# A causal convolution and a token mixer on one core: batch 0's loads, the softmax, the weight casts and the remainder stores

## The chip, the core and the metric

The kernel runs on one core of a Trainium2 chip. That core has a matrix engine (PE, whose weight loads are shown as PEld), a vector engine (DVE), a scalar engine (ACT), GpSimd (POOL), an engine that only issues transfers (SP), and 16 DMA engines that move data between the chip's memory and the core. The metric is device microseconds of one execution; less is better.

## The reference

The input x has 8 batches of 4224 tokens with 192 values each. First comes a causal convolution of 7 taps. Each of 8 heads (24 values each) has its own taps, which are the softmax of its row of `weight`. Then comes a token mixer without softmax:

```
w   = softmax(weight)                      # 8 heads x 7 taps
y   = sum_k w[h,k] * x[s-6+k, h*24:...]    # zeros before token 0
q,k = y @ w_q, y @ w_k                     # 192 -> 64
out = relu((q @ k.T / 8) @ y) @ w_out
```

Since nothing stands between `q @ k.T` and the product with y, the kernel computes `q @ (k.T @ y)`, and `k.T @ y` as `w_k.T @ (y.T @ y)`. With G = y.T y (192 by 192) it forms M = w_k.T G / 8 (64 by 192), and then relu(q M) w_out.

## The kernel before, in words

A batch is cut into two halves of 2112 tokens, and each half into 18 chunks of 122 outputs. A chunk of x lies on 128 partitions (6 tokens of history and 122 tokens), as bf16 in `XW`, which has room for 6 batches. GpSimd issues the loads of x (line 252 for whole chunks, line 273 for the short last chunk), and the DMA converts from float32 on the way. `rows` issues one load of some chunks of one half.

Per batch the stages are:

- Y: the convolution, as a product with a banded matrix per head (`BAND`, line 433), and the evacuation from PSUM to `Y`. `YC` clears the unused rows of the last chunk.
- T: transposes on DVE, 32 by 32 (line 787), and Q: the product with w_q (line 498).
- G: the sum of y.T y over 18 chunks in PSUM bank 7 (lines 526 to 528), its evacuation `GS`, a transposed block (line 546), and MM, which makes M (lines 558 to 563).
- Z: relu(q M), three products of 512 columns for each of 4 blocks of tokens (line 597), and a small remainder of 64 tokens per half (line 600).
- O: the product with w_out (lines 640 and 642; 634 and 635 for the remainder), the evacuation to `OUT`, and the store from SP (line 670). A block's store is 768 KB, the remainder's 96 KB.

PSUM is emptied by ACT or DVE (lines 787 to 795). The order of all this work is written out ahead of time by a planner in the kernel. `KEYS` gives each stage a first key and a width in units of a batch. `CLOCK` holds the times at which the planner takes data to be there: the four groups of batch 0 (`x0`), the band matrix, the weights, and batch 1 onwards (`x`: the first time and the distance between batches). A job that could start now goes by its key; otherwise the job that can start first goes. The planner also decides whether ACT or DVE does each evacuation. On the chip each engine runs its list strictly in order and waits at semaphores, so a job whose data come later than planned holds everything behind it on that engine.

The start is outside the planner: SP loads `weight` spread to 128 partitions (line 282) and w_q (line 288), GpSimd issues batch 0 in four groups of chunks (0 to 2, 3 to 8, 9 to 14, 15 to 17, both halves), 128 partitions compute the same softmax (lines 335 to 345), five predicated copies shift each partition's row of taps to its place (line 358), and four copies write the band (line 371). SP loads w_k and w_out (line 310) behind a wait for batch 0's second group. PE runs 60 matmuls on zeros meanwhile (line 405). The casts of w_k and w_out to bf16 are eight planner jobs (`job_w`), on ACT or DVE. DVE clears the parts of `XW` that loads don't fill, for batches 1 to 5, in two instructions (lines 399 and 400).

Of the kernel before, what the change touches and what calls it, by code (L numbers as in the profile page):

```python
# [14 lines left out]
    "Y": (-1.0, 0.64), "Q": (-0.3, 1.4), "G": (0.06, 0.63), "Z": (0.73, 1.5), "O": (1.59, 0.9),  # L15
# [3 lines left out]
    "x0": (5.0, 6.6, 9.2, 11.6), "band": 6.5, "wq": 6.5, "wk": 11.0, "wo": 12.0, "x": (12.0, 12.0),  # L19
    "store": 5.0, "now": 0.05, "hold": 1.5,  # L20
# [138 lines left out]
def bass_lightweight_conv__then__hypermixer_token_mlp_kernel(  # L159
# [61 lines left out]
    W_F = sbuf("w_f", [128, H, KC], F32)  # L221
    W_MX = sbuf("w_mx", [128, H], F32)
    W_EX = sbuf("w_ex", [128, H, KC], F32)
    W_SM = sbuf("w_sm", [128, H], F32)
    SHIFT = sbuf("shift", [128, H, 56], BF16)
    BITS = sbuf("bits", [128, 1], I32)
# [5 lines left out]
    GROUPS = [[(0, 3), (3, 9), (9, 15), (15, 18)]] + [[(0, 9), (9, 18)]] * (B - 1)  # L232
# [26 lines left out]
    def load(b, c0, c1, grp, deps=()):  # L259
        full = min(c1, NCK - 1)  # L260
        for half in range(2):
            c = c0
            if half == 0 and c == 0:
                rows(b, 0, 0, 16, 128, 1, grp, deps)
                rows(b, 0, 0, 6, 16, 1, grp, deps)
                c = 1
            rows(b, half, c, 0, 128, full - c, grp, deps)
        if c1 == NCK:
            hi = 6 + LAST + (4 if b < B - 1 else 0)
            at = (b * S + (NCK - 1) * CW - 6) * D  # L270
            P.dma(
                "pool",
                lambda e: e.dma_start(
                    XW[0:hi, b % NX, :, NCK - 1, :],
                    bass.AP(x_t, at, [[D, hi], [HALF * D, 2], [1, D]]),
                ),
                grp, list(deps) + z_short[:1] if b == 0 else deps,
            )
# [3 lines left out]
        lambda e: e.dma_start(W_F[:, :, :], bass.AP(w_t, 0, [[0, 128], [1, H * KC]])),  # L282
# [17 lines left out]

    for g, (c0, c1) in enumerate(GROUPS[0]):
        load(0, c0, c1, xg[0][g])
        if g == 0:
            bits = pool(lambda e: e.iota(BITS[:, :], [[0, 1]], base=127, channel_multiplier=-1))

# [11 lines left out]
    for s, (src, wd) in enumerate(((wk_t, DH), (wo_t, D))):  # L317
        wload(2 * s, 0, 128, src, 0, wd, wl[s + 1], [xg[0][1]])
        wload(2 * s + 1, 0, 64, src, 128, wd, wl[s + 1], ())
        wload(2 * s + 1, 64, 128, src, 128, wd, wl[s + 1], ())  # L320


    mask = PS[:, 7, 0:5].bitcast(I32)
    z_mask = []
    for j in range(5):
        z_mask.append(dve(
            lambda e, j=j: e.tensor_scalar(mask[:, j : j + 1], BITS[:, :], j, 1,
# [3 lines left out]

    def bc(ap, n):
        return ap.unsqueeze(2).to_broadcast([128, H, n])

    d = dve(lambda e: e.tensor_reduce(W_MX[:, :], W_F[:, :, :], AX.X, ALU.max), [wg])
    d = dve(
        lambda e: e.tensor_tensor(W_EX[:, :, :], W_F[:, :, :], bc(W_MX[:, :], KC), ALU.subtract),
        [d],
    )
# [63 lines left out]
    def warm(e):  # L403
        for i in range(60):
            last = e.matmul(PS[:, 0, 0:128], WARM[:, :], WARM[:, :], start=True, stop=True)
# [515 lines left out]
```

## Time and profile before

| | |
|---|---|
| median of the runs | 177.39 us (176.98, 177.39, 178.78) |
| the profiled execution, its own time | 179.23 us |
| its span, first to last instruction | 177.5 us |
| busy in the span | PE 86%, ACT 78%, DVE 64%, POOL 27% |
| mean granted clock of PE | 0.943 |
| last matmul's end, last transfer's end | about 165.7 us, about 176.7 us |

The views below count time from the span's start. In a table of stretches each row has a stretch and its length, then the busy time and number of instructions of PE, PEld, DVE, ACT and POOL, then the clock that PE was granted, the mean number of packets in flight per DMA engine (1.00 is one on each of the 16 at all times; it can exceed 1, because an engine holds more than one), and the rate in GB/s. In a timeline each row has a start, a length, the engine ("SPq" is SP issuing a transfer), the line, the operation, its output and input, its shape, how many were merged into the row, and in brackets how long the engine had been idle and what ended that. "x12" is a count.

### The profile page before, as it was taken

How to read it: one execution, taken by the hardware profiler on the slowest of the kernel's cores; microseconds unless marked ns; L12 is line 12 of the kernel's file. 1: busy time of each engine (PE TensorE's matmuls, PEld its weight loads, DVE VectorE, ACT ScalarE, POOL GpSimd, SP SyncE). 2: the span in 40 equal slices, each digit the busy share in tenths (PEclk: the TensorE clock that was granted, in tenths of full speed). 3: DMA queues.
4: the chain of work that ended last, by engine and by line, in shares of the span. 5: the costliest groups of instructions: out<-in, count | busy, mean ns of one | idle time of the engine just before them, and what ended most of it. 6: DMA issues, size and time to landing. Idle time of an engine off the chain costs nothing.

```text
span 177.5 us, 4686 instructions
## 1 busy us (share of the span) xinstructions
PE 152.8 (86%) x1958; PEld 112.8 (64%) x1980; DVE 113.1 (64%) x228; ACT 138.1 (78%) x255; POOL 47.6 (27%) x71
## 2 busy tenths in 40 slices
PE   7739869999999999999999999999599999999300
PEld 7717647667666776677667766776367778766200
DVE  2725828969976686758676867686725863896100
ACT  2346596989999998999899989998767986899400
POOL 7999999999505000000000000000000000000000
PEclk9965978999999999999999999999969999999975
DMA  3999999999999999999999999555640585497980
GB/s 57 130 170 189 206 189 192 190 194 190 261 285 293 262 213 335 250 327 213 329 248 331 216 333 304 199 187 198 219 178 11 215 317 187 158 392 230 388 292 23
DMA packets 48084, 40.38 MB, mean 227 GB/s; under 512 B 37696, under 2 KB 40384, under 8 KB 48064
## 3 DMA queue, kind: packets, MB, share of 16 engines
q0 software_dynamic: 36576, 13.65, 64.7%
q1 hardware_dynamic: 11488, 26.44, 41.3%
q8 instruction: 15, 0.25, 0.5%
q14 instruction: 5, 0.04, 0.1%
HBM read 27.77 MB, written 25.95 MB: 303 GB/s over the span
## 4 chain that ended last, share of the span: by engine, by line
PE 71%; DMA 8%; ACT 7%; issue 3%; POOL 2%; SPq 1%; DVE 1%; ACTq 0%; POOLq 0%
PE ps L640 13%; PE ps L433 11%; PE ps L642 11%; PE ps L597 9%; PE ps L498 8%; PE ps L526 7%; PE ps L527 6%; DMA xw<-in_x_dram 4%; DMA wst<-in_moe_w_out_dram 4%; PE ps L528 4%; POOL xw L252 2%; ACT qt L789 2%; ACT y L789 2%; SPq L310 1%; ACT o_sb L789 1%
## 5 line engine op out<-in xcount | busy, mean ns | idle before, releaser
L789 ACT CAST y<-ps 128x864 bf16<-128x864 f32 (+7 forms) x94 | 50.7, 596 | 8.2 <-PE ps L433 7.9
L789 ACT COPY o_sb<-ps 128x768 f32<-128x768 f32 (+1 forms) x64 | 48.6, 776 | 4.4 <-PE ps L642 3.2
L793 DVE TENSOR_SCALAR zt<-ps 128x512 bf16<-128x512 f32 x54 | 36.8, 683 | 21.6 <-PE ps L597 19.5
L252 POOL DMA_DIRECT2D xw<-in_x_dram x52 | 41.1, 810 | 8.9 <-issue 8.1
L433 PE MATMUL ps<-xw,band 128*128 128x432 bf16 (+2 forms) x144 | 36.1, 354 | 8.6 <-ACT y L789 2.9
L640 PE MATMUL ps<-wo,zt 128*128 128x192 bf16 x256 | 42.5, 248 | 0.3
L642 PE MATMUL ps<-wo,zt 128*128 128x384 bf16 x128 | 41.8, 326 | 0.0
L526 PE MATMUL ps<-y 128*128 128x192 bf16 x144 | 35.6, 254 | 0.9 <-issue 0.2
L787 DVE STREAM_TRANSPOSE yb<-y 128x576 int32<-128x576 int32 x48 | 33.8, 749 | 2.7 <-ACT y L795 2.7
L527 PE MATMUL ps<-y 128*128 128x192 bf16 x144 | 35.4, 254 | 0.0
L640 PEld LDWEIGHTS ps<-wo,zt 128*128 128x128 bf16 x256 | 26.2, 115 | 11.5 <-ACT o_sb L789 3.6
L528 PE MATMUL ps<-y 128*128 128x128 bf16 x144 | 32.4, 225 | 0.0
L597 PE MATMUL ps<-qt,m_sb 128*128 128x512 bf16 x74 | 26.1, 380 | 1.1 <-issue 1.0
L792 ACT ACTIVATE zt<-ps 128x512 bf16<-128x512 f32 x42 | 24.4, 620 | 0.3 <-PE ps L597 0.3
L433 PEld LDWEIGHTS ps<-xw,band 128*128 128x128 bf16 x144 | 12.3, 104 | 16.4 <-ACT y L789 4.6
L527 PEld LDWEIGHTS ps<-y 128*128 128x128 bf16 x144 | 14.6, 101 | 8.4 <-issue 0.7
L526 PEld LDWEIGHTS ps<-y 128*128 128x128 bf16 x144 | 14.6, 102 | 5.4 <-issue 1.1
L789 ACT CAST qt<-ps 128x576 bf16<-128x576 f32 (+1 forms) x21 | 11.7, 585 | 7.2 <-PE ps L498 7.0
L498 PE MATMUL ps<-yb,wq 32*64 32x288 bf16 x768 | 16.0, 294 | 0.5
L789 DVE CAST y<-ps 128x864 bf16<-128x864 f32 (+4 forms) x14 | 10.9, 789 | 8.0 <-PE ps L433 7.8
L789 DVE CAST qt<-ps 128x234 bf16<-128x234 f32 (+1 forms) x27 | 10.3, 414 | 8.1 <-PE ps L498 8.1
L528 PEld LDWEIGHTS ps<-y 128*128 128x128 bf16 x144 | 14.5, 101 | 0.1
(72 smaller groups left out, 121.9 us busy)
## 6 DMA issues: line engine op xcount, KB each, us to landing
out_dram<-o_sb SPq DMA_DIRECT2D x30, 768.0 KB
xw<-in_x_dram POOLq DMA_DIRECT2D x21, 384.0 KB, 27.3
xw<-in_x_dram POOLq DMA_DIRECT2D x7, 432.0 KB, 24.9
out_dram<-o_sb SPq DMA_DIRECT2D x4, 384.0 KB
xw<-in_x_dram POOLq DMA_DIRECT2D x4, 288.0 KB, 7.4
out_dram<-o_sb SPq DMA_DIRECT2D x8, 96.0 KB
xw<-in_x_dram POOLq DMA_DIRECT2D x8, 42.0 KB, 14.7
xw<-in_x_dram POOLq DMA_DIRECT2D x3, 96.0 KB, 7.3
```

The costliest lines, as they stand in the source:

```text
L252: return e.dma_start(XW[lo:hi, b % NX, half, c : c + n, :], bass.AP(x_t, at, [[D, hi - lo], [CW * D, n], [1, D]]),)
L433: last = e.matmul(PS[:, k + j, 0 : 48 * n], BAND[:, h, :], rhs, start=True, stop=True)
L498: last = e.matmul(PS[64 * h : 64 * h + 64, bk + i, 0:288], WQ[r, j, :], rhs, start=j == 0, stop=j == 5, skip_group_check=True)
L526: e.matmul(PS[:, 7, 0:192], y[:, 0:128], y[:, 0:192], start=c == 0, **fl)
L527: e.matmul(PS[:, 7, 192:384], y[:, 256:384], y[:, 192:384], start=False, **fl)
L528: return e.matmul(PS[:, 7, 384:512], y[:, 128:256], y[:, 128:256], start=False, **fl)
L597: return e.matmul(PS[:, bk, :], m[:, parts[k] : parts[k] + 128], q, start=True, stop=True)
L640: e.matmul(o[:, 192 * h : 192 * h + 192], z[:, h, cols], WO1[:, :], start=h == 0, stop=False, **kw)
L642: last = e.matmul(o[:, 0:384], z[:, 2, cols], WO2[:, :], start=False, stop=True, **kw)
L787: return e.transpose(o, i)
L789: return e.copy(o, i) if eng == "act" else e.tensor_copy(o, i)
L793: return e.tensor_scalar(o, i, 0.0, None, op0=ALU.max)
```

## The change

- **Loads of batch 0.** Seven groups, each of one half: chunks 1 to 5 of half 0, chunks 0 to 4 of half 1, chunk 0 of half 0, then 6 to 10, 5 to 9, 11 to 17, 10 to 17. A new job `job_y1` convolves 2, 3, 4 or 8 heads of one half into one PSUM bank. The first half of batch 1's loads is issued ahead of the weight casts, the second half behind them.
- **Softmax.** `weight` is loaded on 8 partitions, one head each; the maximum is subtracted and the sum taken inside the exponential; each head's row is placed in its own column block by a mask, and one matmul with ones spreads the 8 rows to 128 partitions.
- **Weights.** SP's loads of w_k and w_out wait for the fourth new group. The eight casts are GpSimd instructions in its list, no longer planner jobs.
- **Clearing.** `M_SB` is cleared by DVE instead of GpSimd; the unfilled parts of `XW` by GpSimd, batch by batch ahead of that batch's loads, instead of by DVE at once.
- **Filler.** 16 matmuls on zeros ahead of the spreading one and 20 behind it, instead of 60; and in the planner's first 16 us, where it expects PE to be idle for over 0.3 us, matmuls on zeros in a free bank.
- **Stores.** The remainder's store is two transfers of 64 rows, one per half, instead of one of 2 by 64 rows. In the last batch the remainder goes ahead of block 3, and only block 3 is stored in two parts (before: blocks 2 and 3); those parts lie together in `OUT`.
- **Planner.** All `KEYS` and `CLOCK` have new values.

```diff
 KEYS = {
-    "Y": (-1.0, 0.64), "Q": (-0.3, 1.4), "G": (0.06, 0.63), "Z": (0.73, 1.5), "O": (1.59, 0.9),
+    "Y": (-0.83, 0.98), "Q": (-0.34, 1.7), "G": (0.16, 0.5), "Z": (0.87, 1.34), "O": (1.6, 0.8),
 }
 CLOCK = {
-    "x0": (5.0, 6.6, 9.2, 11.6), "band": 6.5, "wq": 6.5, "wk": 11.0, "wo": 12.0, "x": (12.0, 12.0),
-    "store": 5.0, "now": 0.05, "hold": 1.5,
+    "x0": (6.0, 7.2, 7.5, 8.7, 9.9, 11.8, 13.5), "band": 6.2, "wq": 6.5, "wk": 14.5, "wo": 16.5,
+    "x": (18.0, 11.0), "store": 5.0, "now": 0.05, "hold": 1.5, "fill": 16.0,
...
+    W_F = sbuf("w_f", [H, KC], F32)
+    W_MX = sbuf("w_mx", [H, 1], F32)
+    W_EX = sbuf("w_ex", [H, KC], F32)
+    W_SM = sbuf("w_sm", [H, 1], F32)
+    W_EYE = sbuf("w_eye", [H, H], F32)
+    W_ROW = sbuf("w_row", [H, H, KC], BF16)
+    ONES = sbuf("ones", [H, 128], BF16)
...
+    PAIRS = ((0, 1), (2, 3), (4, 5), (6, 7))
+    FOURS = ((0, 1, 2, 3), (4, 5, 6, 7))
+    THREES = ((0, 1, 2), (3, 4, 5), (6, 7))
+    GROUPS = [[
+        ((0,), 1, 6, FOURS), ((1,), 0, 5, FOURS), ((0,), 0, 1, (FOURS[0] + FOURS[1],)),
+        ((0,), 6, 11, FOURS), ((1,), 5, 10, FOURS), ((0,), 11, 18, THREES), ((1,), 10, 18, PAIRS),
+    ]] + [[((0, 1), 0, 9, PAIRS), ((0, 1), 9, 18, PAIRS)]] * (B - 1)
...
-        lambda e: e.dma_start(W_F[:, :, :], bass.AP(w_t, 0, [[0, 128], [1, H * KC]])),
+        lambda e: e.dma_start(W_F[:, :], bass.AP(w_t, 0, [[KC, H], [1, KC]])),
...
+    z_m = dve(lambda e: e.memset(M_SB[:, :, :], 0.0))
+    z_ones = act(lambda e: e.activation(ONES[:, :], WARM[0:H, :], AF.Identity, bias=1.0), [z_warm])
+
+    rows(0, 0, 1, 0, 128, 5, xg[0][0], ())
+    bits = pool(lambda e: e.iota(BITS[:, :], [[1, H]], base=127, channel_multiplier=-1))
+    rows(0, 1, 0, 0, 128, 5, xg[0][1], ())
+    first(0, xg[0][2], z_first)
+    rows(0, 0, 6, 0, 128, 5, xg[0][3], ())
+    rows(0, 1, 5, 0, 128, 5, xg[0][4], ())
+    rows(0, 0, 11, 0, 128, 6, xg[0][5], ())
+    last(0, xg[0][5], z_short)
+    rows(0, 1, 10, 0, 128, 7, xg[0][6], ())
...
-        wload(2 * s, 0, 128, src, 0, wd, wl[s + 1], [xg[0][1]])
+        wload(2 * s, 0, 128, src, 0, wd, wl[s + 1], [xg[0][3]])
...
+    warm(16, [z_warm])
...
+        lambda e: e.tensor_reduce(W_MX[:, :], W_F[:, :], AX.X, ALU.max, negate=True), [wg]
+    )
+    a = act(
+        lambda e: e.activation(W_EX[:, :], W_F[:, :], AF.Exp, bias=W_MX[:, 0:1],
+                               accum_out=W_SM[:, 0:1]),
+        [d],
...
+        lambda e: e.scalar_tensor_tensor(
+            W_ROW[:, :, :], W_EX[:, ::-1].unsqueeze(1).to_broadcast([H, H, KC]), W_SM[:, 0:1],
+            W_EYE[:, :].unsqueeze(2).to_broadcast([H, H, KC]), op0=ALU.mult, op1=ALU.mult,
+        ),
+        [d, eye],
     )
-    a = act(lambda e: e.activation(W_EX[:, :, :], W_EX[:, :, :], AF.Exp), [d])
-    d = dve(lambda e: e.tensor_reduce(W_SM[:, :], W_EX[:, :, :], AX.X, ALU.add), [a])
-    d = dve(lambda e: e.reciprocal(W_SM[:, :], W_SM[:, :]), [d])
+    spread = P.op(
+        "pe",
+        lambda e: e.matmul(PS[:, 6, 0 : H * KC], ONES[:, :], W_ROW[:, :, :], start=True, stop=True),
+        [d, z_ones],
+    )
     d = dve(
-        lambda e: e.tensor_tensor(
-            SHIFT[:, :, 31:38], W_EX[:, :, ::-1], bc(W_SM[:, :], KC), ALU.mult
+        lambda e: e.tensor_copy(
+            SHIFT[:, :, 31:38], PS[:, 6, 0 : H * KC].rearrange("p (h k) -> p h k", h=H)
         ),
-        [d, z_shift],
+        [spread, z_shift],
     )
+    spread = d
...
+    def clear(b):
+        return [
+            pool(lambda e: e.memset(XW[0:6, b, 0, 0, :], 0.0)),
+            pool(lambda e: e.memset(XW[:, b, :, NCK - 1, :], 0.0)),
+        ]
+
+    def load(b, part):
+        old = zero[b] if b < NX else [
+            done[("Y", b - NX, g, k)] for g, q in enumerate(GROUPS[b - NX]) for k in range(len(q[3]))
+        ]
+        if part == 0:
+            first(b, xg[b][0], old)
+            rows(b, 0, 1, 0, 128, 8, xg[b][0], old)
+            rows(b, 1, 0, 0, 128, 9, xg[b][0], old)
+        else:
+            rows(b, 0, 9, 0, 128, 8, xg[b][1], old)
+            rows(b, 1, 9, 0, 128, 8, xg[b][1], old)
+            last(b, xg[b][1], old)
+
+    zero = {1: clear(1)}
+    load(1, 0)
+    warm(20, [])
...
+        tail = b == B - 1 and i == 3
         def then():
             if not rem and q == 0 and not tail:
@@ -658,17 +756,19 @@
             evs = [o for k in range(0 if not tail else q, q + 1) for o in made[("OUT", b, i, k)]]
             at = (b * S + 512 * i) * D
             if rem:
-                src, dims = OUT[:, orr, 0, 0:D], [[HALF * D, 2], [D, 64], [1, D]]
+                parts = [(at + h * HALF * D, [[D, 64], [1, D]], OUT[64 * h : 64 * h + 64, orr, 0, 0:D])
+                         for h in range(2)]
             elif tail:
-                at += 2 * q * D
-                src = OUT[:, orr, :, 2 * D * q : 2 * D * q + 2 * D]
-                dims = [[4 * D, 128], [HALF * D, 2], [1, 2 * D]]
+                parts = [(at + 2 * q * D, [[4 * D, 128], [HALF * D, 2], [1, 2 * D]],
+                          OUT[:, orr, q, :].rearrange("p (h d) -> p h d", h=2))]
             else:
-                src = OUT[:, orr, :, :]
-                dims = [[4 * D, 128], [HALF * D, 2], [1, 4 * D]]
-            st = P.dma(
-                "sp", lambda e: e.dma_start(bass.AP(out_t, at, dims), src), og[orr], evs,
-            )
+                parts = [(at, [[4 * D, 128], [HALF * D, 2], [1, 4 * D]], OUT[:, orr, :, :])]
...
+    def cast(name, o, i, deps):
+        w = pool(lambda e: e.tensor_copy(o, i), deps + [w_ for l in ("wk", "wo") for w_ in made.get(l, [])])
+        w.end = CLOCK[name]
+        made.setdefault(name, []).append(w)
+
+    cast("wk", WK1[:, :, :], twice(WST[:, 0, 0:DH]), [wl[1]])
+    cast("wk", WK2[0:64, 0], twice(WST[0:64, 1, 0:DH]), [wl[1], z_wk2])
+    cast("wk", WK2[64:128, 1], twice(WST[64:128, 1, 0:DH]), [wl[1], z_wk2])
+    cast("wk", WK2[:, 2], twice(WST[:, 1, 0:DH]), [wl[1]])
+    cast("wo", WO1[:, :], WST[:, 2, :], [wl[2]])
+    cast("wo", WO2[0:64, 0:D], WST[0:64, 3, :], [wl[2], z_wo2])
+    cast("wo", WO2[64:128, D : 2 * D], WST[64:128, 3, :], [wl[2], z_wo2])
+    cast("wo", WO2S[:, :], WST[:, 3, :], [wl[2]])
+    load(1, 1)
...
+            idle = t - free["pe"]
+            if 0.3 < idle and t < CLOCK["fill"]:
+                k = min((k for k in range(7) if k not in held and k not in hold),
+                        key=lambda k: banks[k][0])
+                if banks[k][0] + SEE <= free["pe"] + 0.1:
+                    fill(k, int((idle - 0.1) / 0.07), banks[k][1])
...
```

More of the change, by code (lines that the diff above doesn't have):

```diff
@@ L795, in emit, with fill, f @@
         return e.mul(o, i, s) if eng == "act" else e.tensor_scalar(o, i, s, None, op0=ALU.mult)
+    def fill(k, n, deps):
+        def f(e):
+            for _ in range(n):
+                o = e.matmul(PS[:, k, 0:128], WARM[:, :], WARM[:, :], start=True, stop=True)
+            return o
+        P.op("pe", f, deps)
     def place(job, t):
```

182 lines of the change are left out of this document (98 added, 84 removed).

## The prediction

> **What bounds the kernel now.** I read the page first, then tables of stretches, then the places where PE stood still.
>
> ```profile
> span 177.5 us, 4686 instructions
> PEclk9965978999999999999999999999969999999975
> DMA  3999999999999999999999999555640585497980
> q0 software_dynamic: 36576, 13.65, 64.7%
> HBM read 27.77 MB, written 25.95 MB: 303 GB/s over the span
> PE 71%; DMA 8%; ACT 7%; issue 3%; POOL 2%; SPq 1%; DVE 1%; ACTq 0%; POOLq 0%
> ```
>
> The chain of waits is PE for 71%. The clock row has low digits at the start, once near slice 31, and at the end. Stretch by stretch:
>
> ```profile
> 0.00:8.57 8.57, 6.33 (x60) 6.16 (x60) 4.44 (x22) 2.40 (x5) 7.37 (x15) 1.00 0.74 93
> 8.57:12.36 3.79, 0.85 (x9) 0.51 (x9) 1.63 (x3) 2.02 (x8) 3.57 (x10) 0.75 1.38 160
> 12.36:21.46 9.10, 8.94 (x111) 6.92 (x111) 5.68 (x10) 5.59 (x17) 9.10 (x12) 0.73 1.55 197
> 21.46:23.62 2.16, 0.13 (x2) 0.00 (x1) 0.63 (x2) 1.65 (x6) 2.16 (x5) 1.00 1.60 191
> 23.62:30.28 6.66, 6.66 (x89) 4.62 (x89) 3.94 (x8) 5.02 (x8) 6.66 (x9) 0.74 1.60 190
> ...
> 102.53:120.38 17.85, 17.44 (x235) 12.86 (x239) 12.71 (x26) 16.60 (x30) 0.00 (x0) 1.00 0.85 260
> 120.38:142.16 21.78, 19.09 (x238) 13.79 (x241) 12.93 (x26) 16.56 (x30) 0.00 (x0) 0.92 0.44 160
> 126.56:128.73 2.17, 0.00 (x0) 0.03 (x1) 2.13 (x4) 0.86 (x2) 0.00 (x0) 1.00 0.68 237
> 128.73:133.30 4.57, 4.35 (x67) 3.01 (x69) 1.16 (x3) 2.82 (x5) 0.00 (x0) 0.63 0.45 171
> ```
>
> A batch in the middle takes 17.85 us, with PE at 17.44 and ACT at 16.60: both are nearly full at full clock, and new keys have 0.41 us a batch to win at best. The losses lie elsewhere, in three places. (1) The first 30 us. (2) One batch that takes 21.78 us, 3.93 more than its neighbour. (3) The end.
>
> **The end: the remainder's store.** PE is done at 165.7 us and 12 us remain. SP's last issue is one of eight 96 KB stores, of 2 by 64 rows.
>
> ```profile
> 165.43 0.25 PE L635 MATMUL ps<-wo2s,zr 128*128 128x192 bf16 x1
> out_dram<-o_sb SPq DMA_DIRECT2D x8, 96.0 KB
> 171.00:172.00 1.00, 0.00 (x0) 0.00 (x0) 0.00 (x0) 0.00 (x0) 0.00 (x0) 0.50 1.02 369
> 172.00:173.00 1.00, 0.00 (x0) 0.00 (x0) 0.00 (x0) 0.00 (x0) 0.00 (x0) 0.50 0.16 40
> ...
> 175.00:176.00 1.00, 0.00 (x0) 0.00 (x0) 0.00 (x0) 0.00 (x0) 0.00 (x0) 0.50 0.14 47
> 176.00:177.00 1.00, 0.00 (x0) 0.00 (x0) 0.00 (x0) 0.00 (x0) 0.00 (x0) 0.50 0.06 21
> q1 hardware_dynamic: 117, 0.09, 13.1%
> ```
>
> Up to 172 all 16 DMA engines work (1.02). From 172.2 to 176.7 the share is about 0.13, which is 2 engines of 16; the last row is the queue in 174.4 to 176.4, 117 packets and 13.1%. So this store runs on two engines. Every batch has such a store, so these two carry all of that work and lag: at the end by 176.7 − 172.2 = 4.5 us. The change's parts are 64 rows each. Loads of 64 rows exist: those of w_out, two of whose three transfers are of that kind. In the stretch 18.6 to 19.8 SP's queue reads as follows:
>
> ```profile
> q1 hardware_dynamic: 215, 0.14, 49.3%
> ```
>
> That is half of 16 engines, far above 2, so 64 rows spread. The Trainium skill ("DMA: Bandwidth & Descriptors", section "Why a DMA increments its semaphore by 16 and not by 1") says why: a transfer uses the largest number of engines up to 16 that divides the slowest dimension of both sides; 2 gives 2 and 64 gives 16. The trace agrees on the first, at 13.1%.
>
> Spread evenly, the lag of the last two remainders costs 2 × 96 KB at 369 GB/s, about 0.5 us. Gain: 4.5 − 0.5 = **4.0 us**. The bounds are 2.1 us, if only the last remainder's part goes (117 packets, two at a time, in the 2.0 us of that row, and a few more), and 4.5. SP has one more issue per batch:
>
> ```profile
> L670 SPq DMA_DIRECT2D out_dram<-o_sb x42: 372/373/1285, 43.0 to 169.1; - x42
> SPq L670 <- ACT o_sb L789: 118.4, 31, 27.4
> ```
>
> At 0.37 to 1.29 us each, 8 issues lie in 118.4 us that SP waits for evacuations. The remainder ahead of block 3, and block 2 whole, shift bytes within a drain that runs at the full rate either way: zero, with 1.5 us to both sides, since block 2 can be sent later by one evacuation pair.
>
> **The stall in batch 7.**
>
> ```profile
> 126.18 0.38 PE L597 MATMUL ps<-qt,m_sb 128*128 128x512 bf16 x1
> ...
> 128.73 0.53 PE L433 MATMUL ps<-xw,band 128*128 128x432 bf16 x2 [2.17 <-DVE yb L787]
> 56.36 0.69 POOL L273 DMA_DIRECT2D xw<-in_x_dram  x1
> xw<-in_x_dram POOLq DMA_DIRECT2D x1, 33.0 KB, 72.2
> ```
>
> The trace names a DVE transpose as releaser, but the convolution doesn't read it. What it needs is batch 7's last load: issued at 56.36, landed 72.2 us later, at 128.56, just ahead of 128.73. The cost is 2.17 us of idling, and then the clock: 4.57 us at 0.63 is 1.69 us lost. Together 3.86, against 3.93 for the longer batch. The Trainium skill ("TensorE: Matmul & The Clock Gate", section "Why this matters for your kernels") sets the gap that drops the clock at over about 3 us. By that the stall would cost 2.17; the trace shows the clock lost after 2.17, and the measurement decides.
>
> Why so late? DMA's digits fall from 9 to 5 at slice 26 (about 111 us): most engines are through with x by then.
>
> ```profile
> 108.00:112.00 4.00, 3.95 (x79) 2.96 (x78) 3.25 (x6) 3.92 (x8) 0.00 (x0) 1.00 1.10 326
> 112.00:116.00 4.00, 4.00 (x39) 3.04 (x37) 2.34 (x5) 3.78 (x8) 0.00 (x0) 1.00 0.37 125
> ```
>
> From 112 the share is 0.37. The two remainder engines, which serve x and stores in turn, are 17 us behind. Spread, six remainders add 6 × 0.26 (96 KB at 369 GB/s) = 1.6 us to all: x ends at about 113.5. The front (below) brings stores and need 5 us forward. One more 768 KB store ahead of it is 2 us, and the pause in GpSimd's issuing up to 3: at most 118.5, needed at 126.56 − 5 = 121.6 or later, as Y's new keys are later and wider (−0.83 and 0.98 for −1.0 and 0.64). So the stall goes: **3.9 us**.
>
> **The front.**
>
> ```profile
> 7.66 0.87 ACT L371 COPY band<-shift 32x256 bf16<-32x256 bf16 x2 [2.25 <-DVE shift L358]
> 12.36 1.60 PE L433 MATMUL ps<-xw,band 128*128 128x288 bf16 x6 [2.20 <-DMA xw<-in_x_dram]
> 21.92 0.97 ACT L789 CAST wo<-wst 128x192 bf16<-128x192 f32 x3 [1.70 <-DMA wst<-in_moe_w_out_dram]
> 23.62 0.54 PE L433 MATMUL ps<-xw,band 128*128 128x432 bf16 x2 [2.03 <-ACT y L789]
> 28.07 0.69 DVE L789 CAST gs<-ps 128x512 bf16<-128x512 f32 x1 [0.48 <-PE ps L528]
> 30.28 0.22 PE L563 MATMUL ps<-g12t,wk 128*128 128x128 bf16 x1
> ```
>
> The band is ready at 8.53. Softmax: two DVE steps (subtract, sum) go, and a matmul and a copy from PSUM come, which about cancels; `weight` as 8 short rows can land sooner. I take 0.5 us, between −0.3 and 1.5. DVE's clearing of `XW` and GpSimd's of `M_SB` swap engines beside x transfers: nothing.
>
> PE then waits for x until 12.36, because the first groups are small and the second holds both halves. With 640-packet loads first, work goes on from the band. But batch 0's end doesn't come sooner: it is 1.7 MB (13.65 / 8), and with 0.2 MB of weights the early rates (93 GB/s to 8.57, 160 to 12.36, then 197) bring that by 15 us in any order, so the last landing is at about 16.
>
> The second loss is a cast. ACT, in order, waits for w_out until 21.92; evacuations of Y stand behind the casts, PE behind those until 23.62, and the clock is 0.74 for 6.66 us after. G of batch 0 is complete only at 28.07, M's products at 30.28. On GpSimd nothing of PSUM waits for a cast. Behind batch 0's last landing (16) then lie its evacuations, YC, and 8 chunks of G, some 4 us: G at 20, M's products (28.07 to 30.28, 2.2 us later) at 22.3, 8 us sooner. Of these 8, PE had used about 2.5 for batch 1 by 30.28 (10 of its 16 convolution matmuls at 0.18 us, 3 chunks of G at 0.22), work that is still to come: 5.5. I take 1.5 off for the casts' place in GpSimd's list (next): 4, with the band **4.5 us**; range 2 to 8.
>
> What covers this: Z and O of batch 0 (near half of a batch's 17.44 us of PE, by their columns in the code) until batch 1's second half. The eight casts on GpSimd are not shown; bounds from its neighbours:
>
> ```profile
> L379 POOL MEMSET m_sb<- 128x768 bf16 x1 | 0.8, 804 | 0.0
> L396 POOL MEMSET zr<- 128x256 bf16 x1 | 0.3, 306 | 0.0
> ```
>
> 0.31 to 0.80 us each, nearest the smaller by size: 2.5 us (up to 6.4). They wait for w_k and w_out, and behind them in GpSimd's list stand batch 1's second half and all later loads. If w_out lands at 20, those are issued at 21.5 and land at 28, against PE's need at about 30. If it lands at 22, as it did, PE waits 1 to 2 us there, in the range above.
>
> **The sum.** 4.0 + 3.9 + 4.5 = 12.4. The profiled execution's 179.23 becomes 166.8; it stands 1.84 above the runs' median, so 177.39 becomes **165.0 us**.
>
> **The rivals.**
>
> *Loads become the bound at batch 7 (0.18).* x needs 9 us a batch alone (1.7 MB at 190 GB/s, the rate at 23.62) and stores 8.8 (25.95 / 8 MB at 369): 17.8 of 17.85. Against it, the room of six batches and the 3 us of slack above; for it, stores that start sooner share with loads that pause. The front's gain is then waited for again: 177.4 − 4.0 − 3.9 = 169.5.
>
> *The remainder stays on two engines (0.06).* Then terms 1 and 2 stay: 177.4 − 4.5 = 172.9. The w_out loads speak against it.
>
> *The front gives far more (0.10).* If filler keeps the clock up, the losses at 0.73 (2.5 us) and 0.74 (1.7) go too, on top of 4.5, with the keys' share: 160.
>
> *Slower (0.04).* The plan's x times are far ahead of the transfers (11 us apart against 17). If PE, in order, met each of batches 2 to 6 late, as it met batch 7, that is 5 × 3.9 = 19.5 more: 177.4 − 12.4 + 19.5 = 184.5. It decides once loads land behind PE's arrival in more than three batches. Against it: batches 2 to 6 show no such gap now, and the new keys come later.
>
> The forecast has 0.62. About 1% (1.8 us) is what runs of this kernel tell from no change. Faster 0.92, within 0.04 (the first two rivals at once: term 2 stays, the front is waited for again, and nothing is won), slower 0.04. Range 160 to 171: the forecast's own 162 to 168, with the rivals at 169.5 and 160, and 1 us on the far side for the keys.
>
> **What would show it.** The tail: no stretch at a share near 0.13, and the last packet within 7 us of the last matmul (now 11). The stall: no gap of PE over 1 us near batch 7's second half, and the clock at 1.00 from 30 us to PE's end. The front: G's evacuation near 20 and M's products near 22; the casts as POOL rows of 0.3 us; the first w_out product before 30. The forecast is wrong if remainder stores still take 2 engines, if PE waits for x in the middle, or if a batch in the middle takes over 18.2 us.

## The result, and the profile after

| | before | after |
|---|---|---|
| median | 177.94 us (176.98 to 178.78, 4 runs) | 166.19 us (165.51 to 166.91, 4 runs) |
| the profiled execution, its span | 179.23 us, 177.5 us | 165.98 us, 163.9 us |
| last matmul's end to the span's end | 11.8 us | 7.0 us |
| mean granted clock | 0.943 | 0.989 |

The ratio is 0.934, with a 95% interval of 0.927 to 0.941. The forecast was 165.0 us, with a range of 160 to 171. The ratios, here and below, leave out runs over 1.5% above the fastest of their kernel; in one experiment (the remainder's store put back) these are seven of ten, at 179.6 to 182.1 us, so its median lies above what its ratio says.

From the page of the changed kernel: the span, and the rows of the granted clock and of the DMA share in 40 slices.

```profile
span 163.9 us, 4794 instructions
PEclk9999999999999999999999999999999999999995
DMA  3999999999999999999999999999993473678996
```

The clock row has no low digit until the drain; before, it had some in the front and one at slice 30 (about 129 us) too. DMA's digits fall at slice 31 (about 123 us) instead of 26 (about 111 us).

The changed kernel in stretches, with the columns of the earlier tables: the start, the stretches from one transposed block (`GS` turned, line 639) to the next, the last batch, and the drain.

```profile
0.00:6.41 6.41, 4.36 (x37) 3.78 (x38) 4.62 (x23) 2.85 (x7) 5.22 (x12) 1.00 0.72 96
6.41:21.77 15.36, 13.48 (x199) 11.48 (x199) 9.51 (x21) 7.34 (x18) 11.64 (x26) 1.00 1.32 162
...
39.70:58.36 18.66, 18.39 (x244) 13.08 (x243) 15.56 (x30) 16.74 (x31) 15.54 (x22) 1.00 1.39 258
58.36:75.70 17.34, 17.34 (x239) 12.76 (x236) 15.34 (x30) 14.76 (x25) 2.44 (x3) 1.00 1.32 284
75.70:93.38 17.68, 17.68 (x245) 13.10 (x243) 14.45 (x25) 15.70 (x32) 0.00 (x0) 1.00 1.32 282
93.38:110.72 17.34, 17.34 (x238) 12.75 (x236) 15.35 (x30) 14.75 (x25) 0.00 (x0) 1.00 1.32 283
110.72:128.41 17.69, 17.69 (x245) 13.11 (x243) 14.45 (x25) 15.70 (x32) 0.00 (x0) 1.00 0.91 237
128.41:156.87 28.46, 28.19 (x333) 20.67 (x330) 19.86 (x41) 25.15 (x43) 0.00 (x0) 1.00 0.73 274
156.87:163.90 7.03, 0.00 (x1) 0.00 (x0) 0.00 (x0) 0.88 (x2) 0.00 (x0) 0.75 0.77 282
```

Three things are to be read here. The stretch that took 21.78 us takes 17.69, without idling. From 58.36 on the middle batches take 17.34 and 17.68 in turn, 17.51 on average, instead of 17.85, and ACT and DVE are now loaded about evenly (ACT 14.76 and 15.70, DVE 15.34 and 14.45; before, ACT 16.60 and DVE 12.71). And the clock is 1.00 in the whole front. The stretch of 18.66 us ahead of the even ones stands where the kernel before had one of 19.67 (43.96 to 63.63).

The timeline of the changed kernel's PE and GpSimd where the front ends: first convolution, the one wait for x over 1 us, the transposed block, M's last product.

```profile
6.41 0.98 PE L482 MATMUL ps<-xw,band 128*128 128x120 bf16 x8 [0.45 <-ACT band L409]
21.03 0.90 PE L526 MATMUL ps<-xw,band 128*128 128x432 bf16 x4 [1.31 <-DMA xw<-in_x_dram]
21.77 0.22 PE L639 MATMUL ps<-ident,gs 128*128 128x128 bf16 x1
23.14 0.22 PE L656 MATMUL ps<-g12t,wk 128*128 128x128 bf16 x1
```

The timeline of its GpSimd: the casts, and batch 1's second half behind them.

```profile
15.97 1.42 POOL L787 CAST wk<-wst 128x128 bf16<-128x128 f32 x4 [2.27 <-DMA wst<-in_moe_w_k_dram]
17.80 1.24 POOL L787 CAST wo<-wst 128x192 bf16<-128x192 f32 x3 [0.41 <-DMA wst<-in_moe_w_out_dram]
19.39 1.77 POOL L262 DMA_DIRECT2D xw<-in_x_dram  x2
```

The last product of M starts at 23.14 us; before, it started at 30.28 (7.1 us later). A cast on GpSimd costs 0.35 to 0.41 us (1.42 by 4, 1.24 by 3).

The drain, one microsecond a row (same columns):

```profile
158.00:159.00 1.00, 0.00 (x0) 0.00 (x0) 0.00 (x0) 0.00 (x0) 0.00 (x0) 1.00 1.04 406
...
161.00:162.00 1.00, 0.00 (x0) 0.00 (x0) 0.00 (x0) 0.00 (x0) 0.00 (x0) 0.50 1.03 375
162.00:163.00 1.00, 0.00 (x0) 0.00 (x0) 0.00 (x0) 0.00 (x0) 0.00 (x0) 0.50 0.29 103
```

All engines work until 162, and there is no long stretch at 0.13.

### The profile page after: what moved, and what is told of

It is laid out like the page before. It is cut to its first block, busy times and chain, and to the rows that moved or that the text cites. A ratio compares the mean times of both kernels' runs of the same rounds, so it can differ in the third digit from the quotient of the medians.

```text
span 163.9 us, 4794 instructions
## 1 busy us (share of the span) xinstructions
PE 150.9 (92%) x2017; PEld 111.6 (68%) x2017; DVE 122.0 (74%) x241; ACT 129.2 (79%) x235; POOL 51.5 (31%) x86
## 4 chain that ended last, share of the span: by engine, by line
PE 73%; ACT 8%; POOL 7%; DMA 5%; issue 2%; DVE 1%; ACTq 0%; POOLq 0%
PE ps L526 12%; PE ps L733 12%; PE ps L690 11%; PE ps L735 11%; PE ps L591 8%; PE ps L619 7%; PE ps L620 6%; POOL xw L262 5%; DMA xw<-in_x_dram 5%; PE ps L621 4%; ACT o_sb L884 4%; ACT zt L887 2%; ACT y L884 1%; DVE qt L884 1%; PE ps L651 0%
## 5 line engine op out<-in xcount | busy, mean ns | idle before, releaser
L884 ACT COPY o_sb<-ps 128x768 f32<-128x768 f32 (+1 forms) x59 | 45.4, 787 | 7.2 <-PE ps L735 6.5
L884 ACT CAST y<-ps 128x864 bf16<-128x864 f32 (+7 forms) x75 | 42.7, 619 | 6.0 <-PE ps L482 4.2
L888 DVE TENSOR_SCALAR zt<-ps 128x512 bf16<-128x512 f32 x59 | 40.0, 684 | 8.1 <-PE ps L690 7.4
L733 PEld LDWEIGHTS ps<-wo,zt 128*128 128x128 bf16 x256 | 26.9, 114 | 13.0 <-issue 1.6
L619 PE MATMUL ps<-y 128*128 128x192 bf16 x144 | 33.8, 246 | 0.3 <-DVE y L884 0.3
L620 PE MATMUL ps<-y 128*128 128x192 bf16 x144 | 33.7, 246 | 0.0
L690 PE MATMUL ps<-qt,m_sb 128*128 128x512 bf16 x96 | 33.0, 380 | 0.0
L526 PE MATMUL ps<-xw,band 128*128 128x432 bf16 x112 | 29.2, 347 | 2.1 <-DMA xw<-in_x_dram 1.3
L884 DVE CAST y<-ps 128x864 bf16<-128x864 f32 (+10 forms) x33 | 19.7, 628 | 7.1 <-PE ps L526 3.9
L884 ACT CAST qt<-ps 128x576 bf16<-128x576 f32 (+1 forms) x21 | 11.8, 584 | 9.0 <-PE ps L591 9.0
L620 PEld LDWEIGHTS ps<-y 128*128 128x128 bf16 x144 | 14.1, 98 | 6.1
L619 PEld LDWEIGHTS ps<-y 128*128 128x128 bf16 x144 | 14.1, 98 | 5.2 <-issue 1.5
L591 PE MATMUL ps<-yb,wq 32*64 32x288 bf16 x768 | 15.4, 285 | 0.4 <-ACT y L884 0.4
L526 PEld LDWEIGHTS ps<-xw,band 128*128 128x128 bf16 x112 | 9.2, 97 | 7.8 <-DMA xw<-in_x_dram 1.5
L735 PEld LDWEIGHTS ps<-wo,zt 128*128 128x128 bf16 x128 | 14.5, 113 | 0.0
```

Source lines behind the costliest of these rows:

```text
L526: last = e.matmul(PS[:, k + j, 0 : 48 * n], BAND[:, h, :], rhs, start=True, stop=True)
L591: last = e.matmul(PS[64 * h : 64 * h + 64, bk + i, 0:288], WQ[r, j, :], rhs, start=j == 0, stop=j == 5, skip_group_check=True)
L619: e.matmul(PS[:, 7, 0:192], y[:, 0:128], y[:, 0:192], start=c == 0, **fl)
L620: e.matmul(PS[:, 7, 192:384], y[:, 256:384], y[:, 192:384], start=False, **fl)
L690: return e.matmul(PS[:, bk, :], m[:, parts[k] : parts[k] + 128], q, start=True, stop=True)
L733: e.matmul(o[:, 192 * h : 192 * h + 192], z[:, h, cols], WO1[:, :], start=h == 0, stop=False, **kw)
```

## The experiments

The question is which part of the change carries which part of the 11.8 us. "Before" ran beside every group of experiments: 177.79 us (19 runs), 178.14 (7) and 178.30 (7).

### Only the split of the remainder's store

The kernel before, with this edit alone:

```diff
-                src, dims = OUT[:, orr, 0, 0:D], [[HALF * D, 2], [D, 64], [1, D]]
+                parts = [(at + h * HALF * D, [[D, 64], [1, D]], OUT[64 * h : 64 * h + 64, orr, 0, 0:D])
+                         for h in range(2)]
...
```

> The kernel before, with only the remainder's store split into its two halves. Theory (two terms of the sum hang on this edit alone): the tail loses 4.0 us, and batch 7's last load lands near 113 us instead of 128.6, so the gap at 126.6 us and the half clock after it go, another 3.9 us: 177.9 becomes about 170.0. Rival (the edit acts on the tail alone, and batch 7's load is late for another reason): 173.9, with the gap still there. Rival (64 rows don't spread): 177.9.

Measured: 170.81 us (170.01 to 170.99), ratio 0.960 (0.954 to 0.965). In stretches of this kernel, batch 7's and the drain:

```profile
117.29:135.14 17.85, 17.74 (x240) 12.85 (x238) 12.72 (x26) 16.59 (x30) 0.00 (x0) 1.00 0.49 184
161.80:168.80 7.00, 0.00 (x0) 0.00 (x0) 0.36 (x1) 0.72 (x2) 0.00 (x0) 0.85 0.85 300
```

The long batch is gone (21.78 to 17.85, 3.93 us) and the drain is 7.0 instead of 11.8 us (4.8). Both come from one edit. The last load of batch 7 was issued at 56.36 before and took 72.2 us; here its issue and its time to landing are:

```profile
54.10 0.69 POOL L273 DMA_DIRECT2D xw<-in_x_dram  x1
xw<-in_x_dram POOLq DMA_DIRECT2D x1, 33.0 KB, 59.8
```

It is issued at 54.1 and lands 59.8 us later, at 113.9 instead of 128.6. The prediction worked out 113.5 for this. The Trainium skill ("DMA: Bandwidth & Descriptors", section "Why a DMA increments its semaphore by 16 and not by 1") makes the number of engines a matter of the slowest dimension, 2 or 64 here; this experiment agrees: with 64 rows the long stretch at 0.13 is gone, and 7 us with it.

### All but the split

The changed kernel, with the remainder stored in one transfer as before:

```diff
-                parts = [(at + h * HALF * D, [[D, 64], [1, D]], OUT[64 * h : 64 * h + 64, orr, 0, 0:D])
-                         for h in range(2)]
+                parts = [(at, [[HALF * D, 2], [D, 64], [1, D]], OUT[:, orr, 0, 0:D])]
```

> The changed kernel, with the remainder's store as one transfer of 2 by 64 rows again. Theory: the tail is 4 us longer, and x of batch 7, which now lands at 123.5 us, lands some 10 us later on the two engines and stalls PE again (3.9 us or more): 166.2 becomes 174 to 176. Rival (the other edits had already taken the stall away): 170.2, with no gap in PE.

Measured: 180.61 us median (176.06 to 182.07, 10 runs), ratio 0.993 (0.988 to 0.999); the profiled execution took 176.35 us. So without the split all the rest of the change wins about 1% at best, and by the median it wins nothing. The stretches between transposed blocks of this kernel:

```profile
75.20:95.61 20.41, 18.03 (x244) 13.12 (x242) 14.72 (x25) 16.17 (x32) 0.00 (x0) 1.00 1.35 270
95.61:115.26 19.65, 17.64 (x239) 12.74 (x237) 15.64 (x30) 14.63 (x25) 0.00 (x0) 1.00 1.25 261
115.26:135.90 20.64, 18.03 (x244) 13.12 (x242) 14.53 (x25) 16.16 (x32) 0.00 (x0) 1.00 0.50 171
```

And, in its timeline, three of PE's waits (there are six of 0.7 us or more in these stretches, two in each):

```profile
84.57 0.53 PE L526 MATMUL ps<-xw,band 128*128 128x432 bf16 x2 [1.45 <-DMA xw<-in_x_dram]
112.77 0.54 PE L526 MATMUL ps<-xw,band 128*128 128x432 bf16 x2 [1.16 <-DMA xw<-in_x_dram]
125.07 0.53 PE L526 MATMUL ps<-xw,band 128*128 128x432 bf16 x2 [1.90 <-DMA xw<-in_x_dram]
```

Three batches in a row take 2 to 3 us too long, 8.0 in all beside the changed kernel, and the six waits, each ended by a load of x, are 7.0 of it. A faster front brings PE's need for x forward, and the loads that share engines with the unsplit store don't come forward with it: batch 7's last one, issued at 60.91, again takes 72.2 us, to 133.1. This is the mechanism of the prediction's slower rival, in the one variant that keeps the store on two engines.

### Work on PE during batch 7's wait

The kernel before, with 30 matmuls on zeros ahead of the waiting convolution, to separate the stall's idle time from its clock:

```diff
+        if job.name == ("Y", B - 1, 1, 0):
+            def fill(e):
+                for _ in range(30):
+                    o = e.matmul(PS[:, bk, 0:128], WARM[:, :], WARM[:, :], start=True, stop=True)
+                return o
+            P.op("pe", fill, [o for k in held for o in banks[k][1]])
```

> The kernel before, with 30 matmuls on zeros (2 us) ahead of the convolution that waits for batch 7's last load, in its own PSUM banks. The wait for the load stays. Theory (the gap costs 2.17 us of idling and 1.69 us of half clock): the clock row stays at 1.00 after the gap and the time falls by 1.7 us, to 176.2. Rival (the skill's rule, that only gaps over about 3 us drop the clock, so the low clock there has another cause): the clock still drops and the time stays at 177.9.

Measured: 177.52 us (176.94 to 178.57, 10 runs), ratio 0.997 (0.993 to 1.001). The clock did stay up, in the trace of this kernel around the wait:

```profile
126.65 1.84 PE L809 MATMUL ps<-warm 128*128 128x128 bf16 x30
128.33 0.53 PE L433 MATMUL ps<-xw,band 128*128 128x432 bf16 x2
```

The same place in stretches:

```profile
126.50:128.30 1.80, 1.80 (x32) 1.68 (x31) 1.45 (x3) 1.18 (x2) 0.00 (x0) 1.00 0.78 274
128.30:133.00 4.70, 4.70 (x86) 3.40 (x84) 2.81 (x5) 3.51 (x8) 0.00 (x0) 1.00 0.52 195
```

From this convolution to the next transposed block the execution takes 8.68 us (128.33 to 137.01), that of before 10.30 (128.73 to 139.03): in the traces the half clock's 1.6 us are saved, and the profiled execution is 2.0 us shorter (177.22 against 179.23). The median isn't. So the clock did as the theory said, and the time as the rival said. Executions of before differ among themselves, from 177.0 to 180.0 us, and its profiled one, at 179.23, is towards the long end. So the 1.69 us of lost clock are real in the execution that was read, but by the ratio's interval at most 1.2 us of it can be in the median. Whether the other executions of before lose the clock there isn't known, since only one was traced. The two traces differ in more than the edit: this one waits another 1.46 and 0.80 us ahead of batch 7's wait (at 108.0 and 119.7 us, the second for x), where before has no such wait.

### The old keys

The changed kernel with the old `KEYS`, all else as changed:

```diff
-    "Y": (-0.83, 0.98), "Q": (-0.34, 1.7), "G": (0.16, 0.5), "Z": (0.87, 1.34), "O": (1.6, 0.8),
+    "Y": (-1.0, 0.64), "Q": (-0.3, 1.4), "G": (0.06, 0.63), "Z": (0.73, 1.5), "O": (1.59, 0.9),
```

> The changed kernel with the old keys (the planner's times are the new ones). Theory: the new keys brought the middle batches from 17.84 to 17.51 us, about 1.3 us over four batches, and cost 1.8 us in the last one: old keys give 166.2 plus or minus 1, with batches of 17.8 us in the middle. Rival (the old keys ask for Y of batch 7 some 9 us earlier, and x lands at 123.5 us): a gap before batch 7's second half returns, 3.9 us, 170.

Measured: 170.1 us (169.62 to 170.27), ratio 0.956 (0.950 to 0.962). The term that the prediction left out of its sum is 3.9 us. PE doesn't wait for batch 7's x, so it isn't the rival's mechanism either. The middle batches of this kernel, and the one ahead of them:

```profile
58.54:80.15 21.61, 20.89 (x259) 14.38 (x259) 15.42 (x26) 20.06 (x37) 1.23 (x2) 1.00 1.32 281
80.15:98.04 17.89, 17.72 (x240) 12.84 (x238) 12.78 (x27) 16.65 (x30) 0.00 (x0) 1.00 1.32 280
98.04:115.87 17.83, 17.66 (x241) 12.86 (x239) 12.74 (x27) 16.59 (x30) 0.00 (x0) 1.00 1.31 280
115.87:133.73 17.86, 17.69 (x240) 12.91 (x238) 12.74 (x27) 16.59 (x30) 0.00 (x0) 1.00 0.54 190
```

And, in its timeline, a wait near its end:

```profile
159.97 0.35 PE L733 MATMUL ps<-wo,zt 128*128 128x192 bf16 x2 [0.98 <-DVE zt L888]
```

The last three are as long as before the change, with ACT at 16.6 again: 3 × 0.35 = 1.05 us. The wait near the end is 0.98. Part of the other 1.9 us is in the front. The first 30 us, of this kernel and then of the changed one:

```profile
0.00:30.00 30.00, 22.28 (x319) 17.18 (x320) 20.09 (x55) 15.62 (x35) 24.07 (x49) 1.00 1.22 147
0.00:30.00 30.00, 24.96 (x377) 19.84 (x377) 19.50 (x56) 16.71 (x37) 24.50 (x50) 1.00 1.25 152
```

Of PE's busy time 6.05 us here and 7.61 in the changed kernel are matmuls on zeros, so with the old keys PE has done 16.2 us of work by then instead of 17.4, about 1.1 less. The rest wasn't traced. The batch of 21.61 us isn't lost time by its length alone: PE is busy for 20.89 of it, with 259 matmuls instead of 240.

### The new keys without the new front

The kernel before with the split and the new `KEYS` (old loads, old planner times, old softmax, casts on ACT and DVE); beside the split's edit above, this one:

```diff
-    "Y": (-1.0, 0.64), "Q": (-0.3, 1.4), "G": (0.06, 0.63), "Z": (0.73, 1.5), "O": (1.59, 0.9),
+    "Y": (-0.83, 0.98), "Q": (-0.34, 1.7), "G": (0.16, 0.5), "Z": (0.87, 1.34), "O": (1.6, 0.8),
```

> The kernel before with the split remainder and, in addition, the new KEYS alone (old loads, old times in the planner, old softmax, casts on ACT and DVE). With the old KEYS this measured 170.8 us. Theory A: the keys are worth their 3.9 us by themselves, since middle batches become 17.5 instead of 17.85 us long and no batch of over 20 us follows batch 3: about 167 us. Theory B: the keys only let a faster front reach the end, and without the new front they win what the middle batches show, 5 batches of 0.34: 169 us. Theory C (the prediction's term, zero): 170.8 us.

Measured: 172.58 us (171.34 to 174.27), ratio 0.967 (0.961 to 0.974). None of the three: without the new front the new keys win nothing, and by the medians they cost 1.8 us (the intervals of the two ratios, 0.954 to 0.965 and 0.961 to 0.974, just overlap). PE's longest wait in the front of this kernel, from its timeline, and two of its middle batches:

```profile
24.41 2.82 PE L433 MATMUL ps<-xw,band 128*128 128x144 bf16 x10 [2.79 <-ACT qt L795]
80.66:98.72 18.06, 17.41 (x237) 12.81 (x238) 13.40 (x26) 16.86 (x30) 0.00 (x0) 1.00 1.32 280
98.72:116.77 18.05, 17.43 (x235) 12.81 (x238) 13.37 (x26) 16.86 (x30) 0.00 (x0) 1.00 1.08 253
```

ACT is at 16.86, and a batch takes 18.05 instead of 17.85. The wait for ACT in the front is 2.79 us (2.38 with the old keys). How the 1.8 us divides between the two places wasn't measured. With the split in all four, the parts combine like this:

| | old keys | new keys |
|---|---|---|
| old front and planner times | 170.81 | 172.58 |
| new front and planner times | 170.10 | 166.19 |

The lower row also has the casts on GpSimd and the new order of the last stores. The medians come from different groups of runs, whose times of before lie within 0.5 us. Either alone is worth 0.7 or −1.8 us, both together 4.6.

### The old loads of batch 0

The changed kernel with the old four groups of batch 0, both halves each, planner times for them, and w_k and w_out behind the second group as before:

```diff
...
+    GROUPS = [[((0, 1), 0, 3, PAIRS), ((0, 1), 3, 9, PAIRS), ((0, 1), 9, 15, PAIRS),
+               ((0, 1), 15, 18, PAIRS)]] + [[((0, 1), 0, 9, PAIRS), ((0, 1), 9, 18, PAIRS)]] * (B - 1)
...
-    "x0": (6.0, 7.2, 7.5, 8.7, 9.9, 11.8, 13.5), ...
+    "x0": (7.2, 11.0, 13.5, 15.0), ...
...
-        wload(2 * s, 0, 128, src, 0, wd, wl[s + 1], [xg[0][3]])
+        wload(2 * s, 0, 128, src, 0, wd, wl[s + 1], [xg[0][1]])
```

> The changed kernel with batch 0 loaded in the four old groups of both halves (planner's times for them set to their landings, w_k and w_out behind the second group as before). Theory (batch 0's end is set by its bytes, not by their order): at most 1.5 us, 166.2 to 167.7. Rival (the order of the loads is what the front gained by, since PE waits for the second group until 11 to 12 us): 169 to 170.5.

Measured: 173.54 us (171.94 to 174.43), ratio 0.971 (0.963 to 0.980), far outside both. Around the front's end, in its timeline, PE waits twice for x:

```profile
21.89 2.03 PE L526 MATMUL ps<-xw,band 128*128 128x432 bf16 x6 [1.89 <-DMA xw<-in_x_dram]
31.24 0.53 PE L526 MATMUL ps<-xw,band 128*128 128x432 bf16 x2 [3.29 <-DMA xw<-in_x_dram]
```

What GpSimd does meanwhile:

```profile
20.52 1.23 POOL L787 CAST wo<-wst 128x192 bf16<-128x192 f32 x3 [1.58 <-DMA wst<-in_moe_w_out_dram]
22.10 1.77 POOL L260 DMA_DIRECT2D xw<-in_x_dram  x2
```

The stretches behind the two waits (in the first of them the transfers themselves pause, at 52 GB/s):

```profile
21.90:25.70 3.80, 3.80 (x21) 2.63 (x21) 1.74 (x2) 2.49 (x5) 3.50 (x7) 0.55 0.53 52
...
32.46:36.00 3.54, 3.54 (x64) 2.37 (x62) 0.79 (x3) 1.27 (x3) 3.54 (x5) 0.52 1.60 192
```

w_out comes at 20.5 instead of 17.8. Its load is issued once a given group of batch 0 has landed, the second of the old ones (11.7 us) or the fourth of the new (9.6 us), so 2.1 us of this are the groups' order. Batch 1's second half, behind the casts in GpSimd's list, is issued at 22.10 instead of 19.39. The two waits are 5.2 us against 1.3, and behind each the clock is about half for some 3.7 us, 1.7 us lost each time: 3.9 + 3.4 = 7.3. The profiled execution (174.43 us) is 8.5 longer than that of the changed kernel, and two more waits, 0.59 us at 42.7 and 0.70 at 51.8, that the changed kernel hasn't, are near the 1.2 us that remain; between the medians it is 7.4. Here the prediction's "PE waits 1 to 2 us there" comes true, and at a higher price, since the clock goes with it. A version with the old loads and batch 1's loads ahead of the casts, which would take the pause away, wasn't run.

### The casts as planner jobs

The changed kernel with the eight casts as jobs of the planner again, on ACT and DVE:

```diff
-    cast("wo", WO1[:, :], WST[:, 2, :], [wl[2]])
...
     streams = {
+        "W": wjobs,
...
+    x_at = {id(wl[1]): CLOCK["wk"], id(wl[2]): CLOCK["wo"]}
```

> The changed kernel with the eight weight casts as planner jobs on ACT or DVE again (the planner's times of the weights are the new ones, so it expects w_out at about 18 us, near its landing at 17.75). The second half of batch 1's loads then follows the first without a pause. Theory: ACT or DVE do 2.5 us of casts in the front, of which about half shows: 167 to 167.5. Rival (ACT stands still behind w_out again as in the kernel before, with the half clock after it): 169 to 170. Rival (the pause in GpSimd's list cost more than the casts): 165.5.

Measured: 166.7 us (166.07 to 167.12), ratio 0.934 (0.927 to 0.940). Moving the casts is worth 0.5 us, within what separates runs. In the timeline of this kernel's ACT the cast of w_out waits for nothing:

```profile
18.71 0.97 ACT L895 CAST wo<-wst 128x192 bf16<-128x192 f32 x3
```

Before, ACT stood 1.70 us in front of it. The planner's time for w_out was 12.0 and is 16.5 now, near the 17.8 at which the changed kernel starts this cast; w_out also comes sooner (before, the cast waited for it until 21.92). Which of the two takes the wait away wasn't tested by itself.

### The old softmax

The changed kernel with the softmax of before on 128 partitions, without the spreading matmul:

```diff
-        lambda e: e.dma_start(W_F[:, :], bass.AP(w_t, 0, [[KC, H], [1, KC]])),
+        lambda e: e.dma_start(W_F[:, :, :], bass.AP(w_t, 0, [[0, 128], [1, H * KC]])),
...
```

> The changed kernel with the old softmax on 128 partitions, so that the band is ready near 8.5 us instead of 6.4. Theory (batch 0's end is set by its last load): at most 0.7 us, 166.2 to 166.9. Rival (every us of the band's delay is an us of the whole): 168.3.

Measured: 166.7 us (166.53 to 167.25), ratio 0.934 (0.926 to 0.941). The first convolution in its timeline:

```profile
7.89 0.98 PE L467 MATMUL ps<-xw,band 128*128 128x120 bf16 x8 [3.00 <-ACT band L394]
```

The stretches around it:

```profile
4.90:7.90 3.00, 0.01 (x1) 0.01 (x1) 2.25 (x10) 0.88 (x3) 3.00 (x5) 1.00 1.48 189
7.90:14.00 6.10, 6.10 (x79) 5.73 (x79) 3.68 (x11) 3.37 (x8) 5.29 (x12) 0.72 1.54 187
```

It comes 1.48 us later and has the clock at 0.72 behind it, and yet the whole loses 0.5 us, and the transposed block of batch 0 stands at 21.58 us, no later than the 21.77 above. So the band isn't what sets the time of batch 0's transposed block. The 1.3 us by which the profiled execution is longer come later: its next batch takes 19.20 us instead of 17.93, with a wait of 1.23 us for x at 34.1.

### No filler, an earlier load, smaller stores

Three edits of the changed kernel by themselves, and all three together. Without the filler of 20 matmuls and the planner's:

```diff
-    warm(20, [])
...
-                    fill(k, int((idle - 0.1) / 0.07), banks[k][1])
+                    pass
```

> The changed kernel without its filler: the 20 matmuls on zeros behind the spreading one and those that the planner puts into idle time are left out; the 16 at the start stay. Theory (filler is what kept the clock at 1.00 in the first 24 us, where the kernel before had it low twice): the clock row shows a low stretch in the first 25 us and the time rises by 1 to 3.5 us, to 167 to 169.7. Rival (the front waits for loads and evacuations, which don't care for PE's clock): 166.2, with a low clock that costs nothing.

Measured: 165.5 us (164.62 to 165.67), ratio 0.926 (0.919 to 0.933). With both halves of batch 1's loads ahead of the casts:

```diff
     load(1, 0)
+    load(1, 1)
...
-    load(1, 1)
```

> The changed kernel with both halves of batch 1's loads ahead of the eight casts in GpSimd's list, so that the issue of x doesn't pause for w_out. Theory A: the pause (the second half is issued at 19.4 us, DMA share 0.88 around 20 to 24 us) costs something, the prediction took 1.5 us off for it: 164.7 to 165.5 us, and no gap of PE at 19.7 to 21 us. Theory B: the pause is hidden and the w_out casts are what is needed first: 166.2 us, no change. Rival: w_k and w_out share the queue with more x, land later, and PE waits for the casts: 167 us.

Measured: 166.07 us (165.63 to 166.37), ratio 0.933 (0.929 to 0.937). The pause in GpSimd's list is hidden in the changed kernel: PE still waits 1.29 us for batch 1's first half. With all blocks of the last batch stored in halves:

```diff
-        tail = b == B - 1 and i == 3
+        tail = b == B - 1
```

> The changed kernel with all four blocks of the last batch stored in halves (the changed kernel does it for the last block only), so that bytes leave one pair of evacuations earlier. Theory A: the drain behind PE's end runs at the full rate (7.0 us at about 390 GB/s), so bytes sent earlier shorten it; the share in the last batch is 0.73, there is room: 165.2 to 165.7 us. Theory B: SP issues three transfers more, of 0.5 to 1.4 us each at the tail, and it is a wash: 166.2 us.

Measured: 165.91 us (165.44 to 166.62), ratio 0.933 (0.928 to 0.937): a wash. The three edits together:

> The changed kernel without filler matmuls, with both halves of batch 1's loads ahead of the casts and all blocks of the last batch in halves. Leaving the filler out measured 165.5 us. If the three add up: 164 to 164.8 us. If the last two are washes: 165.5 us. If without filler the clock drops in the longer wait for x of batch 0: 167 us.

Measured: 166.52 us (165.62 to 167.81), ratio 0.938 (0.932 to 0.944). None of the four is told apart from the changed kernel, since the intervals overlap; the version without filler has the lowest median, and no gain from filler was seen. The trace of that version, in the stretches of the longest wait and of the front behind it:

```profile
3.73:6.42 2.69, 0.01 (x1) 0.01 (x1) 2.28 (x8) 0.84 (x2) 2.69 (x5) 1.00 1.40 177
6.42:21.88 15.46, 12.60 (x162) 10.59 (x163) 9.63 (x21) 7.36 (x18) 11.71 (x26) 1.00 1.33 161
```

PE stood 2.69 us and the clock stayed at 1.00.

## Why the prediction was right, and where it wasn't

**The tail** was set at 4.0 us, between 2.1 and 4.5. The drain became 4.8 us shorter, with the split alone as with the whole change. The mechanism holds; the size was 0.8 short, and 0.3 beyond the bound. Behind PE's end all engines worked for about 6.4 us before and about 5.5 with the split alone; the sum had left this part as it was. Why it is shorter wasn't pursued.

**The stall** was set at 3.9 us, and in the profiled executions 3.93 went, by the split alone. Between the medians it is less: tail and stall together are 8.7 us between the profiled spans (177.5 and 168.8) and 7.0 between the medians. If the tail's 4.8 hold there too, 2.2 are left for the stall, about its idle part. The difference of 1.7 is near the 1.84 by which the profiled execution of before stood above its median. The prediction took these 1.84 off the time and left the gain of 12.4, all of it read from that execution, as it was. In medians the parts are 7.0 and 4.6, 0.8 less than 12.4; that it is no more has some luck in it, as the tail's 0.8 make up for half of the stall's 1.7.

In the whole change the step "at most 118.5" failed: batch 7's last load was issued at 61.33 and took 62.2 us, so it landed at 123.5.

```profile
61.33 0.69 POOL L278 DMA_DIRECT2D xw<-in_x_dram  x1
xw<-in_x_dram POOLq DMA_DIRECT2D x1, 33.0 KB, 62.2
```

PE didn't wait, since its need came later as well: by the order of the convolutions in the trace, the one that waits for this load starts at 125.71. With the old keys the same load landed at 118.0. The rival of loads that become the bound did not come about, but the slack was 2.2 us instead of 3.

**The front** was set at 4.5 us (range 2 to 8), and the size is right: 170.81 − 166.19 = 4.6. In the two traces the last product of M comes 7.1 us sooner (8 in the forecast), and PE's end 4.9 (161.8 and 156.87). But the working is wrong in three places, and their errors cancel: without the new keys, which it gave nothing, the front is worth 0.7. That the size came out is luck.

- "On GpSimd nothing of PSUM waits for a cast" was given as the main cause. The casts' engine is worth 0.5 us. With the new planner times and the casts on ACT, ACT doesn't stand in front of w_out either; the step took the engine for the cause, where a later planned time and an earlier w_out were enough.
- That "batch 0's end doesn't come sooner" in any order is true of the last landing (15.4 us, about 16 in the forecast) but was the wrong thing to ask. The order decides when w_k and w_out land and when batch 1 is issued behind the casts, and with the old groups the same kernel loses 7.4 us.
- "New keys have 0.41 us a batch to win at best" was the ground for giving them no term in the sum. With the new front they are worth 3.9, without it −1.8. The middle batches did win only 0.34 us each, under that bound; the bound was on the wrong quantity, as about a quarter of the keys' worth shows in the middle, and about as much in the first 30 us. It also rested on PE's busy time, 17.44 of 17.85 with 235 matmuls; with the split alone a batch of the same length shows 17.74 with 240, so part of that idling was matmuls missing from the record.

The band's 0.5 us was right, by the softmax experiment. The 1.5 us taken off for the casts' place in GpSimd's list weren't due in the changed kernel (0.1 by the experiment that moves the loads ahead), and were too little with the old loads. The transposed block behind G's evacuation and the last product of M came at 21.8 and 23.1, for G at 20 and M at 22.3.

**The rivals and the signs.** The remainder did go to all engines: no stretch at 0.13 is left. One stretch, 39.70 to 58.36, takes 18.66 us, over the 18.2 that the prediction named as a sign against it; it has one of 19.67 at its place before, and those behind it are 17.34 to 17.69. The front's clock stayed up, as the rival of 160 us wanted, but without filler it stays up as well, and it didn't bring 5 us more. The slower rival's waits appeared in the version without the split, which the prediction put at 172.9 with a front that keeps its 4.5: measured, 176.35 us in the profiled execution and 180.6 in the median.

**What stays open.** What turns the middle batches from ACT-heavy (16.6 of 17.85) to even isn't settled. The versions with the old loads, the casts as jobs and the old softmax all have the short batches, in turn 17.34 and 17.7; the version with old keys and the one with the old front don't. All that do have the new keys, the planner's new times and the changed order of the last stores; the new keys with those alone weren't run.

## What to carry to other kernels

A transfer that few DMA engines carry needn't show at its own place alone: look for loads on another queue that land late in the same engines, and mend the transfer before anything that brings the work forward. Where an order is planned ahead, the keys and the front that the plan expects belong together; here the keys alone cost 1.8 us and with the new front were worth 3.9, so test them together and undo one at a time from the end. And a term whose size comes out right can still have the wrong cause: the version with that one part undone tells.

## What the runs showed of the hardware

The clock doesn't follow one length of a wait. It was lost after 1.89 us (old loads, at 21.9 us: 0.55), 2.17 (before, batch 7: 0.63) and 3.00 us (old softmax: 0.72), and kept after 2.69 us at the start (no filler), 1.90 us in batch 7 (without the split, 1.00 over that stretch) and 1.70 us in the front (matmuls in batch 7's wait, 1.00 from 22.6 to 28.0 us). The Trainium skill ("TensorE: Matmul & The Clock Gate", section "Why this matters for your kernels") names gaps of over about 3 us; these runs show it lost after shorter ones, and they don't show what decides.
